# An explicit order of issue and a table of buffers in place of a planner (linear attention times an FFN gate, one core)

## The chip, the core and the metric

The kernel runs on one core of a Trainium2 chip. The metric is the device time of one execution in microseconds (us), median of the runs. A profile of one execution gives the start and the duration of every instruction on the engines: PE (TensorE; PEld is its weight load), DVE (VectorE), ACT (ScalarE), POOL (GpSimd) and SP (SyncE, which issues the DMAs), and the clock that TensorE was granted.

## The reference

```python
S, D, H, Dh, F = 2048, 512, 32, 16, 1792
xn = layernorm(x)
q, k, v = split(xn @ wqkv)                      # 32 heads of 16
phi_q = concat(softmax(q @ w_phi), softmax(-q @ w_phi))   # per head, 32 features
phi_k = concat(softmax(k @ w_phi), softmax(-k @ w_phi))
kv = einsum("bhsf,bhsd->bhfd", phi_k, v);  z = einsum("bhsf->bhf", phi_k)
o = (phi_q @ kv) / (phi_q @ z + 1e-6)
s = o @ wo
h = xn @ w1 + b1
g = silu((h * tanh(softplus(h))) @ w2)          # Dense, Mish, Dense
return x + s * g
```

## The kernel before

All data are float32. A product is done as three matmuls of a faster 4-byte type (fp32r): each operand is split into a high and a low part (names ending in h and l, as wv0h and wv0l), and low·high, high·low and high·high are summed. The large products go by a seven-product scheme for 2×2 blocks (Strassen and Winograd), so that DVE, POOL and ACT form sums of blocks of the operands ahead of the matmuls and of the products behind them.

Names that the text uses: x0 to x15 are the 16 tiles of 128 rows of the input. wkT and wqT are the transposed k and q weights, loaded in parts (wkT00, wkT01, wkT10, wkT11; wqT10, wqT00); wkf and wqf are those folded with w_phi on PE, and they go through ACT and DVE (wkh, wkl) before use. wvr0 and wvr1 are the v weights; wv0h/wv1h (ACT) and wv0l/wv1l (POOL) their parts; phic and phit the w_phi matrix. pt is a transpose of a normalised tile on PE, fh and fl its parts. kx, ky, kz, kj are products of the k and v stage; kvp the sum of phi_k·v (128 small matmuls a block); qx, qy products of the q stage; pn the numerators (115 or 116 small matmuls a block); den and f the denominators; fx, fy, fz products of the first FFN matrix (weights w1al, w1ah, w1sh and others, formed from w1a; w1b are parts that were stored to memory and are loaded again); pw the product with wo, so its result in memory; y70 to y74 and others the products of the second FFN matrix (weights w2h, w2l, w2g, w2m, w2t; operands ah, al split from r, the Mish output's blocks and sums). At the end DVE forms yc and u from y, ACT applies silu, DVE multiplies with sr (the rows of s, loaded from so) and adds xx (the rows of x, loaded again), and SP issues the stores to out.

The code does not call the engines directly. Every operation is recorded as an `Op` with its readings and writings and, for each engine that can do it, an implementation. `ORDER` is a list of parts (N4 is the norm of tile 4, wv0 the weights wv0, Fa12 a quarter of FFN block 12, Q6 a q block and so on) and fixes the order of PE's work. `Program.order` gives each operation a due time from that order, with `SHIFT` as corrections for single operations, and `Program.simulate` walks through a model of the engines with costs (`cost`), DMA rates and buffer counts, choosing for each operation when it is issued and, where several engines can do it, on which. `Program.issue` then emits everything in the order of the starts that this model gave; this is the line that carries nearly every instruction (line 404 in the kernel before, line 293 in the changed one). Each engine works off its own queue in that order, with semaphores between the engines; SP's queue is one of these, so a DMA that waits for its buffer holds those behind it.

Buffers come from pools that rotate: 8 PSUM banks, 38 slots of 4 KB per partition, 15 of tag s2, and smaller ones. Which buffer a name gets follows from the order in which the planner gives them out. For operations on POOL issued shortly after a DVE operation with two operands in SBUF, `issue` adds a dependency on it, named "port".

Of the kernel before, what the change touches and what calls it, by code (L numbers as in the profile page):

```python
# [17 lines left out]
P = 128  # L18
# [10 lines left out]
PEN, HOLD, MARGIN, GUARD = 0, 300, 1000, 140  # L29
BACK, COLD, DRATE, LANES, SWITCH = 2650, 3400, 400, 8, 230  # L30
READ, WRITE, STALL, AHEAD_PE = 1150, 150, 1500, 110
BLOCK, HEAD, FETCH, IDLE = 256, 89, 5200, 2100
BEGIN = {"PE": 1100, "V": 900, "G": 2300, "A": 800, "Q": 800}

SLOTS, S2 = 38,15
SLACK, AHEAD, LAT = 15000, 40000, 150
WAKE, EACH, NEAR = 15, 2, 4000
# [11 lines left out]
SHIFT = """  # L49
kd:0:-9100 wv1:0:-1100 N1:2:-15000 N1:3:300 N1:5:5800 N1:13:4300 N1:14:-7000 kl:3:-10000 Ka2:3:-9700 N5:6:-2200  # L50
N5:8:-1200 N5:11:13000 N2:0:-3500 N2:2:-2000 N3:4:1500 N3:13:-11400 Kc0:7:4900 Kc0:10:14200 k4:0:-6900 Kd0:6:300
N6:14:-6700 P0:1:4800 P0:5:3800 P0:11:5000 Kb1:3:300 N7:6:-2800 N7:8:7300 N7:9:-6400 N8:8:-2700 N9:13:3600 Kc1:8:1800
Kd1:4:-7300 N10:3:-300 N11:0:5800 P4:0:-7000 P4:4:300 P4:5:3100 N14:8:-6800 Kd3:1:-5000 Kd3:6:-6400 A2:0:-3600
N13:5:-2500 Fa4:1:-1100 Fa4:3:3600 N15:4:10800 N15:6:-5000 N15:11:-300 Kc5:6:4400 Ka6:1:-600 Kc6:5:-300 Kc6:6:2600
P6:6:-1100 P6:8:5100 P3:3:-2600 P3:11:-2000 Kb7:1:2800 Fa3:1:-300 Fa3:3:300 P2:4:-2000 P2:6:1100 P2:10:800 Kd6:6:-8800
Kd6:9:-9500 Fb6:3:-2300 Fc3:1:1600 Fc3:2:800 Fc3:4:7900 wQ:1:2300 wQ:13:6600 Fa2:3:300 Fa2:4:-1900 Fa1:3:900
M4:1:-1400 P5:10:3200 Q0:7:14700 Q0:23:-2000 z:4:1200 z:5:11100 D0:0:800 D0:4:4700 D0:8:-800 L:5:-4200 L:9:-3000
D1:2:-8100 Q1:16:800 Q1:19:300 Q2:3:-15000 Q2:9:-2500 Q2:15:300 Q2:25:-1900 Q3:17:-4300 Q3:18:4700 Fc5:5:9400
D3:7:1800 D4:3:-4000 D4:4:6800 D4:5:1300 D4:6:11900 D4:10:11500 D5:1:-300 Fb11:1:-4700 Q4:7:-600 Q4:16:600 Q4:18:7800
Q4:20:800 Q4:21:-1400 Q4:23:-8800 Q5:25:-600 M3:1:-5000 M3:2:-6700 Fa12:1:800 D6:6:-500 D6:10:300 Fb10:1:-500  # L60
D7:1:5000 D7:4:6600 D8:1:-2400 D8:4:-500 D8:10:1400 Q6:1:4700 D9:10:800 Q7:1:7800 Q7:16:-4700 Q7:20:4800 Q7:21:-13000
Q7:23:-12900 M2:2:-5000 D10:6:-800 M6:2:-4100 D11:1:-1700 Ua0:1:-1100 Ua0:12:-800 Fc9:1:3400 D12:5:-5000 D13:0:-4400
D13:4:12500 Fa13:4:800 Ub0:14:-4300 wo0:1:-4500 Fc13:4:-13100 Fc7:2:15000 R0:8:4700 D14:6:-7800 O3:2:-900 Ua1:2:-4200
Ua1:4:-6700 Ua1:6:-3100 Ua1:11:-5000 Ua1:13:-300 Ua1:14:300 O5:2:-500 Fd13:2:-4200 O6:1:-2200 Ub1:5:-5000 Ub1:6:-2000
Ub1:8:-4500 G7:4:-2000 R2:0:-2200 R1:1:15000 R1:6:4200 R1:10:5800 G8:3:-5000 G8:6:1900 O11:2:-2000 R6:1:4900 R3:2:1600
R3:8:-3300 R4:1:2000 G11:0:-6800 G12:5:3100 G12:6:-1200 G13:5:-1100 G32:3:6500 G34:6:4000 G1:4:-15000 G3:0:5000
G4:0:-4100 G5:5:4000 G35:3:9300 G35:4:-5800 G35:6:3100 G14:0:-10200 G14:3:4000 E0:6:-2600 G15:2:800 G39:6:-300
G16:4:-5000 G41:3:1700 E5:4:-300 G20:0:800 G20:2:-2000 G20:3:-5300 G20:6:-5000 G42:3:5100 G42:5:-300 G43:2:4200
G44:2:300 G44:4:-2000 H4:2:1300 G46:3:6600 G46:6:300 G24:6:500 G47:5:-3000 G26:4:-1600 E6:2:-800 G49:0:-5000
G49:2:4000 G49:6:-1100 G49:9:2000 G49:12:-2200 G49:19:2200 G49:26:5000 G49:31:800 G49:36:2800 G49:42:-4700 G49:43:800  # L70
E7:9:-300 E7:10:15000 H3:7:2300 H6:8:800
"""
ACT_SET = {AF.Exp: 1, AF.Silu: 3, AF.Mish: 2}


class Op:
    __slots__ = ("impl", "reads", "writes", "at", "idx", "succ", "ndep", "late", "new", "ready", "start", "eng", "sets", "slack", "open", "soon", "pos", "deps", "lock", "part", "half", "code", "tiles", "shift")


class Program:  # L80


    def __init__(self, nc):
        self.eng = {"PE": nc.tensor, "V": nc.vector, "G": nc.gpsimd, "A": nc.scalar, "Q": nc.sync}
        self.ops, self.tag, self.cap, self.pe = [], {}, {}, []
        self.group, self.slack, self.part, self.half = None, SLACK, None, False
        self.region, self.count = {}, {}
        self.shifts = {k: int(v) for k, _, v in (c.rpartition(":") for c in SHIFT.split())}

    @staticmethod  # L90
    def cost(e, m, a, k):
        aps = [v for v in a if isinstance(v, bass.AP)]
        n = aps[0].free_size()
        if e == "PE":
            if m == "transpose":
                return 109
            n, c = aps[2].free_size(), aps[1].free_size()
            if aps[1].dtype == F32R:
                return max(n / 2.4 + 0.104 * c, c * 0.835 + 2)
            full = 2 * max(n / 1.2 + 2.5, c * 0.835)  # L100
            if aps[1].shape[0] == 32:
                return max(0.155 * n, 24)
            return max(full * aps[0].shape[0] / P, 27)
        if e == "Q":
            return 450
        if e == "A":
            return (60 if aps[1].space == "PSUM" else 110) + 0.833 * n + 93 * sum(isinstance(v, bass.AP) for v in k.values())
        psum = any(v.space == "PSUM" for v in aps[1:])
        nn = max(v.free_size() for v in aps)
        if e == "V":  # L110
            if m == "reciprocal":
                return 70 + 6.3 * n
            if m in ("tensor_scalar", "tensor_copy") and not psum:
                return 70 + 0.52 * n
            return 70 + 1.04 * nn
        if k.get("op") == ALU.pow:
            return 520
        return (140 + 1.73 * n) if bcast(a) else (140 + 2.17 * n)

    @staticmethod  # L120
    def records(m, a, k):

        return 2 if m == "transpose" or a[1].dtype == F32R else 4
# [11 lines left out]
    def add(self, impl, reads, writes, sets=()):  # L135
        o = Op()
        o.tiles = {n.split("#")[0] for n in reads | writes}
        o.code = sum(self.records(*c) for c in impl["PE"][1]) if "PE" in impl else 0
        o.impl, o.reads, o.writes, o.idx, o.sets, o.slack = impl, reads, writes, len(self.ops), sets, self.slack
        o.pos, o.part, o.half = len(self.pe), self.part, self.half  # L140
        self.half = False
        key = self.part or "@"
        n = self.count[key] = self.count.get(key, -1) + 1
        o.shift = self.shifts.get(f"{key}:{n}", 0)
        o.lock = {e for e, (_, calls) in impl.items() if any(locks(e, m, a) for m, a, k in calls)}
        if "PE" in impl:
            self.pe.append(o)
        self.ops.append(o)

    def call(self, e, m, a, k):  # L150
        aps = [v for v in list(a) + list(k.values()) if isinstance(v, bass.AP)]
        w = self.names(aps[0]) - {"out"}
        r = set().union(*map(self.names, aps[1:]))
        c = self.cost(e, m, a, k)
        s = [ACT_SET[a[2]]] if e == "A" and a[2] in ACT_SET else []
        if self.group is None:
            self.add({e: (c, [(m, a, k)])}, r, w, s)
        else:
            g = self.group
            g[0].setdefault(e, [0, []])  # L160
            g[0][e][0] += c
            g[0][e][1].append((m, a, k))
            g[1].update(r)
            g[2].update(w)
            g[3].extend(s)

    def halves(self):

        self.group[0]["PE"][0] += SWITCH
        self.half = True  # L170

    @contextmanager
    def one(self):
# [4 lines left out]
        self.group = ({}, set(), set(), [])  # L178
        yield
        g, self.group = self.group, None  # L180
        self.add({e: tuple(v) for e, v in g[0].items()}, g[1], g[2], g[3])

    def order(self):
        at = [0]
        for o in self.pe:
            at.append(at[-1] + o.impl["PE"][0])
        self.links()
        return self.simulate(at)

    def links(self):  # L190
        ops = self.ops
        wr, rd, head = {}, {}, {}
        for o in ops:
            o.succ, dep = [], {head.setdefault(n, o.idx) for n in o.tiles if self.tag.get(n, "ps") != "ps"}
            for n in o.reads:
                dep.update(wr.get(n, ()))
                if self.tag.get(n) == "ps":
                    dep.update(rd.get(n, ()))
            for n in o.writes:
                dep.update(wr.get(n, ()))  # L200
                dep.update(rd.get(n, ()))
# [1038 lines left out]
```

## Time and profile before

| what | value |
|---|---|
| time, median of 3 runs | 489.14 us (489.06 to 489.71) |
| profiled execution, span | 488.7 us |
| profiled execution, whole time | not listed beside its span; the median is 0.44 us above the span |
| granted TensorE clock | 1.00 of full speed |
| PE / DVE / ACT / POOL busy | 480.2 / 446.2 / 293.4 / 267.2 us |
| DMA | 105.70 MB, mean 216 GB/s |

PE's records overlap (one begins before the last has drained), so durations of single matmuls exceed their spacing: the matmuls of 512 columns start 0.23 us apart, six of them 1.36 us, though each record shows 0.39. "Idle before" in brackets is the time in which an engine had nothing to do ahead of an instruction, and the arrow names what ended it.

### The profile page before, as it was taken

Reading aid. Unit: us, or ns where it says so; the run is one execution under the profiler, and the core shown is the slowest. Engines: PE = TensorE matmul, PEld = TensorE weight load, DVE = VectorE, ACT = ScalarE, POOL = GpSimd, SP = SyncE. Lnnn points to the kernel's source line nnn. Section 1 sums busy time; section 2 is a strip of 40 time slices with the busy share of each in tenths; the row PEclk is TensorE's granted clock in tenths of the full one; section 3 lists DMA queues with packets and bytes.
Section 4 is the critical chain, followed back from the end, with each engine's and each line's share of the span. In section 5 each row is a group of like instructions: output and inputs, shape, how many; then the busy total and the mean of one; then the engine's idle time right before and its main releaser. Section 6 shows DMA issues by size and latency. Waiting matters only on the chain.

```text
span 488.7 us, 10325 instructions
## 1 busy us (share of the span) xinstructions
PE 480.2 (98%) x3820; PEld 426.2 (87%) x3820; DVE 446.2 (91%) x893; ACT 293.4 (60%) x453; POOL 267.2 (55%) x197
## 2 busy tenths in 40 slices
PE   8899999999999999999999999999999999999996
PEld 7788888888887889898887878788899999999996
DVE  6999999988899999999999899889989889999894
ACT  3997545654556453635345545677879687777631
POOL 3989998998490446798987686370021024120030
PEclk9999999999999999999999999999999999999999
DMA  8812923968867689982959635726465646578172
GB/s 294 265 48 109 332 99 122 312 197 272 315 217 313 225 301 345 394 300 87 310 199 341 229 115 211 261 85 207 141 193 165 201 154 211 194 234 269 44 250 94
DMA packets 68641, 105.70 MB, mean 216 GB/s; under 512 B 6896, under 2 KB 37744, under 8 KB 68592
## 3 DMA queue, kind: packets, MB, share of 16 engines
q1 hardware_dynamic: 68448, 104.79, 62.9%
q8 instruction: 30, 0.49, 0.4%
q10 hardware_dynamic: 144, 0.26, 0.2%
q14 instruction: 19, 0.16, 0.1%
HBM read 60.60 MB, written 44.43 MB: 215 GB/s over the span
## 4 chain that ended last, share of the span: by engine, by line
PE 81%; DVE 8%; DMA 5%; issue 2%; ACT 1%; SPq 1%; POOL 1%; DVEq 0%; ACTq 0%
PE y L404 20%; PE fx L404 14%; PE pw L404 9%; PE kx L404 7%; PE fy L404 7%; PE qx L404 5%; PE ky L404 3%; PE fz L404 3%; PE qy L404 2%; PE kj L404 2%; PE pn L404 2%; PE kz L404 2%; DVE al L404 2%; DMA wvr<-wv 1%; DMA w1a<-w 1%
## 5 line engine op out<-in xcount | busy, mean ns | idle before, releaser
L404 POOL TENSOR_TENSOR al<-r,ah 128x896 fp32r<-128x896 f32 x8 | 17.0, 2130 | 87.4 <-DMA r<-hd 35.1
L404 ACT ACTIVATE ah<-r 128x896 fp32r<-128x896 f32 x56 | 50.9, 944 | 16.0 <-DVE r L404 12.9
L404 DVE TENSOR_TENSOR al<-r,ah 128x896 fp32r<-128x896 f32 x48 | 54.8, 1171 | 5.0 <-ACT ah L404 3.2
L404 DVE TENSOR_TENSOR r<-r 128x128 f32<-128x128 f32 (+1 forms) x157 | 48.3, 353 | 5.0 <-ACT r L404 3.4
L404 PE MATMUL y<-w2h,al 128*128 128x256 f32 x160 | 45.4, 283 | 0.0
L404 PE MATMUL y<-w2h,ah 128*128 128x256 f32 x160 | 45.3, 283 | 0.0
L404 PE MATMUL y<-w2l,ah 128*128 128x256 f32 x160 | 45.3, 283 | 0.0
L404 PE MATMUL y<-w2t,ah 128*128 128x256 f32 x224 | 41.0, 283 | 0.0
L404 PE MATMUL fx<-fh,w1b 128*128 128x512 f32 x112 | 38.8, 393 | 0.0
L404 ACT ACTIVATE r<-r 128x512 f32<-128x512 f32 x56 | 33.2, 621 | 7.9 <-DMA r<-hd 7.9
L404 PEld LDWEIGHTS y<-w2t,ah 128*128 128x128 f32 x224 | 34.9, 192 | 0.0
L404 PE MATMUL y<-w2t,al 128*128 128x256 f32 x112 | 31.7, 283 | 0.0
L404 PEld LDWEIGHTS y<-w2h,al 128*128 128x128 f32 x160 | 30.7, 192 | 0.6 <-issue 0.4
L404 PEld LDWEIGHTS y<-w2l,ah 128*128 128x128 f32 x160 | 30.7, 192 | 0.2
L404 PEld LDWEIGHTS y<-w2h,ah 128*128 128x128 f32 x160 | 30.7, 192 | 0.0
L404 PE MATMUL y<-w2g,ah 128*128 128x256 f32 x160 | 30.4, 283 | 0.0
L404 PEld LDWEIGHTS fx<-fh,w1b 128*128 128x128 f32 x112 | 21.0, 188 | 5.4 <-issue 1.2
L404 PEld LDWEIGHTS y<-w2g,ah 128*128 128x128 f32 x160 | 25.0, 192 | 0.0
L404 POOL TENSOR_TENSOR r<-r 128x128 f32<-128x128 f32 (+1 forms) x11 | 6.4, 592 | 32.3 <-DMA sr<-so 22.5
L404 PE MATMUL y<-w2g,al 128*128 128x256 f32 x80 | 22.6, 283 | 0.0
L404 ACT ACT_TABLE_LOAD x13 | 16.7, 1283 | 9.2 <-DMA x<-x 4.1
L404 PE MATMUL fx<-fl,w1b 128*128 128x512 f32 x56 | 21.8, 390 | 0.0
(766 smaller groups left out, 1730.0 us busy)
## 6 DMA issues: line engine op xcount, KB each, us to landing
r<-hd SPq DMA_DIRECT2D x56, 256.0 KB, 3.5
xd<-xc SPq DMA_DIRECT2D x8, 896.0 KB, 4.1
w1b<-w1d SPq DMA_DIRECT2D x14, 512.0 KB, 5.5
w1b<-w1d SPq DMA_DIRECT2D x14, 384.0 KB, 4.9
so<-so SPq DMA_DIRECT2D x16, 256.0 KB, 2.1
x<-x SPq DMA_DIRECT2D x15, 256.0 KB, 3.7
w1a<-w SPq DMA_DIRECT2D x7, 512.0 KB, 4.6
w1d<-w1sh SPq DMA_DIRECT2D x7, 512.0 KB, 2.9
```

The source lines that it names most:

```text
L404: ins = getattr(e, m)(*a, **k)
```

## The change

The planner (`cost`, `links`, `simulate`, the due times, `SHIFT` and all its constants) is removed. In its place stand two tables. `PLAN` names all 2455 operations, in the order in which they are issued, on all engines, PE and DMA included; an operation is its part and its number in the part, with a letter where several engines can do it (V for DVE, A for ACT, G for POOL). `PLACE` names the PSUM bank or the SBUF slot of each buffer, so the pools don't rotate: each slot is a pool entry of its own. The tables come from a search in which transfers land late at random. The "port" dependency is added where at most 24 operations, not 4000 ns of the model's time, lie between the DVE operation and the one on POOL, and not for DMAs. What is computed, and the set of instructions on PE, is the same.

```diff
-PEN, HOLD, MARGIN, GUARD = 0, 300, 1000, 140
...
-WAKE, EACH, NEAR = 15, 2, 4000
+WAKE, EACH, NEAR = 15, 2, 24
...
-SHIFT = """
-kd:0:-9100 wv1:0:-1100 N1:2:-15000 N1:3:300 N1:5:5800 N1:13:4300 N1:14:-7000 kl:3:-10000 Ka2:3:-9700 N5:6:-2200
...
+PLAN = """
+N4.0 N1.0 @.0 @.15 @.1 N4.3 @.2 @.17 @.3 N0.0 @.4 wv0.0 @.5 @.18 @.6 @.7 N4.1 @.19 @.8 @.9 N1.1 wv1.0 @.10 @.16G @.11
...
     def order(self):
+        at = {o.name: o for o in self.ops}
+        plan = []
+        for c in PLAN.split():
+            e = c[-1] if c[-1] in self.eng else ""
+            o = at.pop(c[:-1] if e else c)
+            o.eng = e or next(iter(o.impl))
+            plan.append(o)
...
     def issue(self, tc):
         first, held = True, None
-        for o in self.order():
-            for i, (m, a, k) in enumerate(o.impl[o.eng][1]):
+        for n, o in enumerate(self.order()):
+            for i, (m, a, k) in enumerate(o.impl[o.eng]):
...
-                if i == 0 and o.eng == "G" and held is not None and o.start - held[1] < NEAR:
+                if i == 0 and o.eng == "G" and m != "dma_start" and held is not None and n - held[1] < NEAR:
```

Of the 2677 rows of PE 1407 stand at the same place in both. DVE goes from 876 rows to 866, ACT from 456 to 453, POOL from 201 to 222, SP from 311 to 312. 63 operations move from DVE to POOL, 41 from POOL to DVE, 12 from ACT to DVE and 9 from DVE to ACT.

Three places follow. The first is the start of the program, on SP (the loads) and on PE. SP before:

```order
L404 DMA x4_151<-x 128x512
L404 DMA x5_153<-x 128x512
L404 DMA phic_100<-phi 128x64
L404 DMA x0_164<-x 128x512
L404 DMA wkT00_137<-wqkT 128x512
L404 DMA wkT01_138<-wqkT 128x512
L404 DMA wvr0_141<-wv 128x2x512
L404 DMA wkT10_139<-wqkT 128x512
L404 DMA wvr1_159<-wv 128x2x512
L404 DMA wkT11_140<-wqkT 128x512
```

SP after:

```order
L293 DMA x1_170<-x 128x512
L293 DMA phic_100<-phi 128x64
L293 DMA x5_153<-x 128x512
L293 DMA wkT00_137<-wqkT 128x512
L293 DMA x0_164<-x 128x512
L293 DMA wvr0_141<-wv 128x2x512
L293 DMA wkT01_138<-wqkT 128x512
L293 DMA wkT10_139<-wqkT 128x512
L293 DMA wvr1_159<-wv 128x2x512
L293 DMA wkT11_140<-wqkT 128x512
```

The same transfers stand ahead of wkT11; wkT00 and wvr0 moved forward, wkT01 back, and x1 and x4 changed places (the other of the two is the first DMA of all, on ACT's queue). PE at the same place, before (the first rows after `wake`):

```order
L404 MATMUL wkf01_147<-phit_101,wkT00_137 128x128 x4
L404 MATMUL wkf11_148<-phit_101,wkT01_138 128x128 x4
L404 MATMUL pt4_156<-ident_83,x4_151 128x128 x4
L404 MATMUL pt0_167<-ident_83,x0_164 128x128 x4
L404 MATMUL pt1_173<-ident_83,x1_170 128x128 x4
L404 MATMUL wkf21_181<-phit_101,wkT10_139 128x128 x4
L404 MATMUL wkf31_182<-phit_101,wkT11_140 128x128 x4
L404 MATMUL pt5_184<-ident_83,x5_153 128x128 x4
L404 MATMUL kx2_187<-wv0h_142,fl00_104 128x512
```

PE after:

```order
L293 MATMUL wkf01_147<-phit_101,wkT00_137 128x128 x4
L293 MATMUL pt1_173<-ident_83,x1_170 128x128 x4
L293 MATMUL pt4_156<-ident_83,x4_151 128x128 x4
L293 MATMUL wkf11_148<-phit_101,wkT01_138 128x128 x4
L293 MATMUL pt0_167<-ident_83,x0_164 128x128 x4
L293 MATMUL pt5_184<-ident_83,x5_153 128x128 x4
L293 MATMUL wkf21_181<-phit_101,wkT10_139 128x128 x4
L293 MATMUL wkf31_182<-phit_101,wkT11_140 128x128 x4
L293 MATMUL kx2_187<-wv0h_142,fl00_104 128x512
```

The transposes moved ahead of the folds of the late wkT parts. Behind kx2 (six matmuls) before come kz2 (six), wqf21, wqf31 and kj00; after come wqf21, kz2, kj00 (twelve), kj03 (six) and then wqf31.

The second place is DVE around w1al2, a part of the weights of FFN block 2. DVE before:

```order
L404 TENSOR_TENSOR w1s1_462<-w1a1_461,w1s1_462 128x256
L404 TENSOR_TENSOR k14e_475<-k14e_475,k14r_472 128x1024
L404 TENSOR_TENSOR w1s2_498<-w1a2_497 128x256
L404 TENSOR_TENSOR w1sl1_466<-w1s1_462,w1sh1_465 128x1024
L404 TENSOR_TENSOR w1al2_500<-w1a2_497,w1ah2_499 128x768
```

DVE after:

```order
L293 TENSOR_REDUCE k14m_474<-k14p_471 128x32
L293 TENSOR_TENSOR k14e_475<-k14m_474,kx7_421 128x32x16
L293 TENSOR_TENSOR w1al2_500<-w1a2_497,w1ah2_499 128x768
L293 TENSOR_REDUCE k15m_450<-k15p_446 128x32
L293 TENSOR_TENSOR k12e_460<-k12m_459,kx6_408 128x32x16
L293 TENSOR_TENSOR w1s1_462<-w1a1_461 128x256
```

w1al2 moved ahead of the sums w1s1 and w1sl1. In the order of issue its first reader on PE (fx2) came next behind it; now three groups of six matmuls come between them.

The third place is the end of DVE's queue. Before:

```order
L404 TENSOR_TENSOR yc4_1181<-yc2_1179,y71_1167 128x256
L404 TENSOR_TENSOR yc4_1181<-yc4_1181,sr13_1_1183 128x256
L404 TENSOR_TENSOR xx13_1_1182<-yc4_1181,xx13_1_1182 128x256
L404 TENSOR_TENSOR u13_0_1187<-yc2_1179,y72_1168 128x256
L404 TENSOR_TENSOR u13_0_1187<-u13_0_1187,sr13_0_1186 128x256
L404 TENSOR_TENSOR xx13_0_1185<-u13_0_1187,xx13_0_1185 128x256
L404 TENSOR_TENSOR u15_1_1190<-yc3_1180,y73_1169 128x256
L404 TENSOR_TENSOR u15_1_1190<-u15_1_1190,sr15_1_1189 128x256
L404 TENSOR_TENSOR xx15_1_1188<-u15_1_1190,xx15_1_1188 128x256
L404 TENSOR_TENSOR u15_0_1193<-u15_0_1193,sr15_0_1192 128x256
L404 TENSOR_TENSOR xx15_0_1191<-u15_0_1193,xx15_0_1191 128x256
```

After:

```order
L293 TENSOR_TENSOR u13_0_1187<-yc2_1179,y72_1168 128x256
L293 TENSOR_TENSOR u13_0_1187<-u13_0_1187,sr13_0_1186 128x256
L293 TENSOR_TENSOR yc4_1181<-yc2_1179,y71_1167 128x256
L293 TENSOR_TENSOR u15_1_1190<-yc3_1180,y73_1169 128x256
L293 TENSOR_TENSOR yc4_1181<-yc4_1181,sr13_1_1183 128x256
L293 TENSOR_TENSOR xx13_0_1185<-u13_0_1187,xx13_0_1185 128x256
L293 TENSOR_TENSOR u15_1_1190<-u15_1_1190,sr15_1_1189 128x256
L293 TENSOR_TENSOR xx13_1_1182<-yc4_1181,xx13_1_1182 128x256
L293 TENSOR_TENSOR xx15_1_1188<-u15_1_1190,xx15_1_1188 128x256
L293 TENSOR_TENSOR u15_0_1193<-u15_0_1193,sr15_0_1192 128x256
L293 TENSOR_TENSOR xx15_0_1191<-u15_0_1193,xx15_0_1191 128x256
```

u13_0 moved ahead of yc4 and its product with sr13_1. On PE the block y72 moved ahead of y70 and y71; on SP the load of sr13_1 moved from 6 rows ahead of the end to 18.

More of the change, by code (lines that the diff above doesn't have):

```diff
@@ L1 @@
 from contextlib import ExitStack, contextmanager
-import heapq
 import numpy as np
@@ L55 @@
[L55 to L59, printed above, removed]
@@ L76 @@
+"""
+PLACE = {
+    "ps": """
[4 rows of a table added]
+""",
+    "s2": """
[4 rows of a table added]
+""",
+    "slot": """
[11 rows of a table added]
+""",
+    "sm": """
[3 rows of a table added]
+""",
+    "tq": """
+1 0 1 0 0 1 0 1 0 1
+""",
+    "rq": """
+7 6 1 5 4 2 3 0 7 6 5 2 1 4 0 3
+""",
+}
 class Op:
-    __slots__ = ("impl", "reads", "writes", "at", "idx", "succ", "ndep", "late", "new", "ready", "start", "eng", "sets", "slack", "open", "soon", "pos", "deps", "lock", "part", "half", "code", "tiles", "shift")
+    __slots__ = ("impl", "reads", "writes", "idx", "name", "eng", "lock")
 class Program:
@@ L84, in __init__ @@
         self.eng = {"PE": nc.tensor, "V": nc.vector, "G": nc.gpsimd, "A": nc.scalar, "Q": nc.sync}
-        self.ops, self.tag, self.cap, self.pe = [], {}, {}, []
-        self.group, self.slack, self.part, self.half = None, SLACK, None, False
+        self.ops, self.tag = [], {}
+        self.group, self.part = None, None
         self.region, self.count = {}, {}
[L88 to L123, printed above, removed]
     def names(self, v):
@@ L133, in names, with add @@
         return {f"{n}#{where(int(e))}" for e in np.unique(at // 128) * 128}
-    def add(self, impl, reads, writes, sets=()):
+    def add(self, impl, reads, writes):
         o = Op()
[L137 to L141, printed above, removed]
         key = self.part or "@"
         n = self.count[key] = self.count.get(key, -1) + 1
[L144 to L147, printed above, removed]
+        o.impl, o.reads, o.writes, o.idx, o.name = impl, reads, writes, len(self.ops), f"{key}.{n}"
+        o.lock = {e for e, calls in impl.items() if any(locks(e, m, a) for m, a, k in calls)}
         self.ops.append(o)
@@ L408, in issue @@
             if o.eng == "V" and "V" in o.lock:
-                held = ins.ins.name, o.start + o.impl["V"][0]
+                held = ins.ins.name, n
 def locks(e, m, a):
@@ L473, in alloc @@
     def alloc(tag, shape, name, dtype=F32):
-        t = pools[tag].tile(shape, dtype, tag=tag, name=name)
+        t = pools[tag].tile(shape, dtype, tag=tag if tag == "st" else tag + next(place[tag]), name=name)
         prog.tag[t.tensor.name] = tag
```

400 lines of the change are left out of this document (143 added, 257 removed), and 22 rows, old and new, of the table PLACE.

## The prediction

> **What bounds the kernel now.** I read the page's busy line first, then the windows, the waits of PE, and the timelines of the stretches in which PE sat idle.
>
> ```profile
> PE 480.2 (98%) x3820; PEld 426.2 (87%) x3820; DVE 446.2 (91%) x893; ACT 293.4 (60%) x453; POOL 267.2 (55%) x197
> ```
>
> PE is busy for 480.2 of 488.7 us. Both kernels issue the same set of PE instructions, so reordering can only win PE's 8.5 us of idle time, or lose by making new idle time. DVE at 91% is the second bound. The windows (busy us of PE, PEld, DVE, ACT, POOL, then clock, DMA share, GB/s) say where the idle time is:
>
> ```profile
> 0.00:10.00 10.00, 8.00 (x51) 7.41 (x52) 5.70 (x22) 2.58 (x3) 3.92 (x13) 1.00 0.77 269
> 10.00:20.00 10.00, 8.39 (x57) 7.11 (x57) 9.34 (x23) 9.00 (x20) 8.30 (x5) 1.00 0.97 305
> 20.00:140.00 120.00, 120.00 (x799) 99.73 (x799) 109.84 (x210) 76.12 (x120) 106.01 (x78) 1.00 0.59 201
> 140.00:160.00 20.00, 19.73 (x325) 15.96 (x324) 19.97 (x27) 12.15 (x17) 6.00 (x4) 1.00 0.78 286
> 260.00:280.00 20.00, 20.00 (x205) 15.89 (x204) 18.41 (x45) 9.77 (x18) 13.01 (x9) 1.00 0.79 278
> 280.00:300.00 20.00, 20.00 (x205) 15.89 (x204) 19.23 (x42) 11.34 (x21) 15.37 (x11) 1.00 0.52 184
> 300.00:320.00 20.00, 20.00 (x296) 15.50 (x296) 17.66 (x32) 11.90 (x23) 10.06 (x12) 1.00 0.59 201
> 475.00:488.70 13.70, 9.13 (x77) 8.93 (x75) 5.84 (x14) 1.52 (x4) 0.00 (x0) 1.00 0.36 126
> ```
>
> PE is idle for 2.00 and 1.61 us in the first two rows, 0.27 us at 140 to 160, 4.57 us in the tail, and nowhere else. The clock is 1.00 throughout. The waits of PE name the releasers:
>
> ```profile
> PE wake L404 <- DVE mhalf L527: 1.1, 1, 1.1
> PE wkf L404 <- DMA wkT<-wqkT: 1.0, 2, 0.7
> PE wqf L404 <- ACT wqf L404: 0.7, 1, 0.7
> PE pt L404 <- DVE x L404: 0.6, 2, 0.4
> PE fx L404 <- DVE w1al L404: 0.3, 1, 0.3
> PE kz L404 <- POOL wv1l L404: 0.2, 1, 0.2
> ```
>
> The wait of `wake` is the program's start and stays. The rest, 2.8 us, is what a better order of issue can address; the tail comes on top.
>
> **The start.** In PE's timeline (start, duration, then the group) and, in the last two lines, POOL's and ACT's:
>
> ```profile
> 10.81 1.13 PE L404 MATMUL wkf<-phit,wkT 128*128 128x128 f32 x8
> 12.67 1.16 PE L404 MATMUL wkf<-phit,wkT 128*128 128x128 f32 x8 [0.73 <-DMA wkT<-wqkT]
> 13.66 0.60 PE L404 MATMUL pt<-ident,x 128*128 128x128 f32 x4
> 14.02 0.48 PE L404 MATMUL kx<-wv0h,fl 128*128 128x512 f32 x1
> 15.47 0.39 PE L404 MATMUL kz<-wv1h,fl 128*128 128x512 f32 x1
> 16.06 0.50 PE L404 MATMUL kz<-wv1l,fh 128*128 128x512 f32 x1 [0.20 <-POOL wv1l L404]
> 17.32 1.05 PE L404 MATMUL wqf<-phit,wqT 128*128 128x128 f32 x8
> 19.06 1.16 PE L404 MATMUL wqf<-phit,wqT 128*128 128x128 f32 x8 [0.69 <-ACT wqf L404]
> 19.97 0.48 PE L404 MATMUL kj<-wv0h,fl 128*128 128x512 f32 x1
> 13.60 2.40 POOL L404 TENSOR_TENSOR wv1l<-wvr,wv1h 128x1024 fp32r<-128x1024 f32 x1
> 12.10 1.07 ACT L404 ACTIVATE wv1h<-wvr 128x1024 fp32r<-128x1024 f32 x1
> ```
>
> The fourth wkf (wkf31) starts when wkT11 lands, about 12.6. In SP's new order the loads issued ahead of wkT11 are the same ones, in another sequence (x0 and wvr0 have moved ahead of wkT01, x1 and x4 have swapped queues), so I keep 12.67. From there the new PE order is wkf31, kx (6), wqf21, kz (6), kj00, with pt5 already done during the wait and wqf31 put off. From the starts above, wkf takes 13.66 − 12.67 = 0.99, kx 15.47 − 14.02 = 1.45 and wqf about 19.97 − 19.06 = 0.91. That puts kz at 12.67 + 0.99 + 1.45 + 0.91 = 16.02, wv1l being needed one matmul later, at 16.25. POOL finished it at 16.00 before; now it is no later, since wvr0 is loaded ahead of wkT01 and ACT's wv1h has the same place. With kz at 1.36 (the usual six, below) and 0.1 for the return from a wqf, kj00 starts at 17.5. One wqf (0.91) is still owed, so equal work stands at 18.4 against 19.97: **−1.6 us**. The two recovered waits (0.69, 0.20), pt5's 0.36 out of the path, and the gap in kz's row (16.06 − 15.47 − 0.23 = 0.36) account for most of it. I put the bounds at −0.8 (wkT11 or wv1l later by about the 0.73 that wkf waited before) and −2.4 (wkT11 earlier by as much).
>
> **Passages between kinds of matmul.** The chain of waits shows what follows a block of small matmuls:
>
> ```profile
> 38.38 1.36 PE ky L404 x6
> 102.72 1.93 PE kvp L404 x128
> 104.65 1.59 PE kx L404 x6
> ```
>
> Six large matmuls behind kvp take 1.59 where the usual six take 1.36: 0.23 for a passage. In the order of issue the returns from kvp/pn go from 7 to 8 and those from wkf/wqf from 1 to 4, those from pt from 9 to 8. The first costs +0.23; a return from wqf or pt costs the 0.09 by which kx takes 1.45 and not 1.36, so +0.27 − 0.09. Together +0.4, of which 0.2 is already in the start (the 1.45 and the 0.1): **+0.2 us**. Ends: 0 (PE catches up at the next wait) and 0.6.
>
> **The wait for w1al.** At 150 us PE's fx waited 0.3 us for DVE's w1al2. In PLAN three groups of six matmuls (4.1 us at 1.36) stand between w1al2 and its first reader, where there was none: **−0.3 us**; ends −0.4 and 0 (DVE, busy 19.97 of 20 there, is late with the next thing).
>
> **The tail.** DVE's last rows, and ACT's last:
>
> ```profile
> 480.99 0.43 DVE L404 TENSOR_TENSOR yc<-yc,sr 128x256 f32<-128x256 f32 x1 [3.17 <-DMA sr<-so]
> 484.85 0.42 DVE L404 TENSOR_TENSOR xx<-u,xx 128x256 f32<-128x256 f32 x1
> 485.19 0.42 DVE L404 TENSOR_TENSOR u<-u,sr 128x256 f32<-128x256 f32 x1
> 485.65 0.42 DVE L404 TENSOR_TENSOR xx<-u,xx 128x256 f32<-128x256 f32 x1
> 484.27 0.36 ACT L404 ACTIVATE u<-y 128x256 f32<-128x256 f32 x1
> ```
>
> The last u·sr could start at 484.27 + 0.36 + 0.03 = 484.66, but DVE is late with its queue until 485.19, since one block waited 3.17 us for the load of sr13_1. In the new SP order this load stands 18 rows from the end instead of 6, and y72 is computed before y71, so that u13_0 leaves the queue before the last two y blocks are ready. Six DVE operations of about 0.42 are left behind the last but one y block, and PE's last block takes 21 × 0.12 = 2.5 us: they just fit. **−0.5 us**; ends −0.55 and 0.
>
> **DVE and POOL.** 63 operations leave DVE for POOL and 41 come the other way, 7 of the 8 `al` of POOL among the latter. I priced both lists with the mean of each form's group: DVE gains about 7 us over the kernel, POOL loses 10, ACT 0.7. I cost this at nothing, since PE waits once for DVE outside the start; the cover is DVE's idle time, and the thin place is 260 to 320 us. There the new DVE list has about 8 us more ahead of the same PE matmuls, while DVE's idle time in the three rows is 1.59 + 0.77 + 2.34 = 4.7 us. So what is uncovered is between 0 (a list that runs ahead earlier pays it before 260) and 3.3 us. I take 0, because up to 260 the new list stands level with the old one or ahead of it, and in 20:140 DVE has 10 us of idle time and never held PE. Rows on how DVE and POOL meet:
>
> ```profile
> L404 DVE TENSOR_TENSOR al<-r,ah x48: 1079/1085/3228, 312.8 to 463.1; 128x896 fp32r<-128x896 f32 x48
> L404 POOL TENSOR_TENSOR al<-r,ah x8: 2121/2130/2137, 363.9 to 464.4; 128x896 fp32r<-128x896 f32 x8
> L404 POOL TENSOR_TENSOR r<-r x11: 454/508/751, 308.5 to 436.1; 128x128 f32<-128x128 f32 x6, 128x256 f32<-128x256 f32 x5
> ```
>
> The longest `al` on DVE is 3.228 us, its usual 1.085 plus one POOL `al` (2.13). The Trainium skill, page "SBUF — State Buffer", section "SBUF: two separate sides", calls the port pair that the two engines share an exclusive lock: whichever starts first holds it for the whole instruction and the other fully blocks. The row agrees with it (3.23 against 1.09 + 2.13). By that rule the short `r` that now go to POOL would block DVE more often and for shorter. In rows: 22 more POOL operations at 0.508 us are 11.2 us of POOL time; if a quarter of it stopped a DVE operation, DVE would lose 2.8 us, and the seven `al` that leave POOL give back up to 2.13 each. So I leave it out of the sum.
>
> **The sum.** −1.6 + 0.2 − 0.3 − 0.5 = −2.2 us on a span of 488.7, so 486.5. The median of the runs, 489.14, is 0.44 above this span, which I take as the time around it: **486.9 us**.
>
> **The rivals.**
> - *The start isn't moved* (no change): wkT11 and wv1l land as much later as wkf waited before (0.73), and the wait takes back the start. Against it: the loads ahead are the same. 489.14 − 0.3 − 0.5 + 0.2 = 488.5.
> - *DVE becomes the bound at 260 to 320 us* (no change to slower): if 2.2 us of the 3.3 are uncovered the whole gain is gone, and PE shows waits for den, f or ol. With the full 3.3 it gives 486.9 + 3.3 = 490.2. It decides from 3.2 us on. For it: DVE at 19.23 of 20 in 280 to 300. Against it: the windows on either side have room.
> - *A reload comes late* (slower): w1b35, a part of the first FFN matrix, now goes into the buffer that the last qx/qy products of Q6 read, and stands ten rows behind its sister w1b25 in SP's queue, not directly behind. From the last reader to its first use PE has four groups of 1.36 and some qx/qy, about 6.2 us.
>
> ```profile
> DMA to landing us min/median/max: 2.9/5.3/9.2
> ```
>
>  This row is w1b's loads from issue to landing. At the median of 5.3 it is in time; at 9.2 PE waits 3.0 us: 489.9. It is slower than no change from a landing of 9.4 on, and takes the gain from 8.4.
> - *More than summed*: the start at −2.4 and nothing paid for passages: 485.9.
>
> **How the numbers follow.** About 0.2% (1 us) is what a measurement of this kernel can tell from no change. Chances: the forecast 0.48 (own range 486.2 to 487.9); more than summed 0.14; the start not moved 0.12, in the same band; DVE 0.16, half of it in the band and half above; the late reload 0.10, half and half. Faster is thus 0.62 and a little of the start's case, 0.64; same 0.22; slower 0.14. The range leaves out about one in ten on each side: from 485.6 (below the largest gain) to 490.0 (most of DVE's and the reload's).
>
> **What would show it.** Right: PE's windows 0:20 idle for about 2 us instead of 3.6, kj00's first row near 17.5, no wait of wqf for ACT; no fx waiting for w1al; DVE's last u·sr straight behind ACT's last u; PE at 20.00 of 20 from 20 to 475 us. Wrong: rows in PE's waits with DVE den, f, ol or w2 between 260 and 330, or fx waiting for DMA w1b near 250; wkf waiting over 1.4 us for wkT in all. What would make the prediction wrong most easily is DVE: its list is longer, and I have only bounded how that meets PE.

## The result and the profile after

The changed kernel takes 485.82 us (median of 4 runs, 485.75 to 486.15) against 489.25 us (4 runs, 489.06 to 489.71): a ratio of 0.9932, 95% interval 0.9918 to 0.9946. It is 3.4 us faster; the forecast was 486.9, that is 2.2 us faster.

The page's busy line after:

```profile
PE 478.1 (99%) x3820; PEld 426.1 (88%) x3820; DVE 444.5 (92%) x874; ACT 286.7 (59%) x450; POOL 262.7 (54%) x219
```

PE does the same 3820 matmuls in 2.1 us less "busy" time. Busy time thus contained waits; the reading beforehand had missed this. The windows (columns as before) and PE's waits:

```profile
0.00:10.00 10.00, 7.87 (x49) 7.62 (x50) 5.75 (x22) 3.22 (x5) 3.99 (x13) 1.00 0.83 289
10.00:20.00 10.00, 10.00 (x65) 8.93 (x64) 9.90 (x26) 8.78 (x20) 9.15 (x6) 1.00 1.09 379
140.00:160.00 20.00, 20.00 (x213) 16.78 (x212) 19.39 (x25) 10.69 (x16) 6.85 (x8) 1.00 0.77 255
260.00:280.00 20.00, 20.00 (x213) 15.62 (x216) 19.14 (x43) 12.23 (x22) 13.93 (x9) 1.00 0.73 252
280.00:300.00 20.00, 20.00 (x205) 16.09 (x205) 19.41 (x44) 8.96 (x20) 13.73 (x11) 1.00 0.66 232
300.00:320.00 20.00, 20.00 (x331) 15.70 (x330) 18.63 (x40) 12.99 (x28) 7.49 (x10) 1.00 0.52 178
```

```profile
PE wake L293 <- DVE mhalf L394: 1.1, 1, 1.1
PE pt L293 <- DVE rs L293: 1.0, 1, 1.0
```

The waits of wkf, wqf, kz and fx are gone; pt waits once for the norm. PE is never idle from 10 to 475 us, although DVE is fuller than before between 260 and 320 us (57.2 us busy against 55.3). The start and the end in the timeline after:

```profile
9.19 0.66 PE L293 MATMUL pt<-ident,x 128*128 128x128 f32 x4 [1.01 <-DVE rs L293]
11.52 1.95 PE L293 MATMUL wkf<-phit,wkT 128*128 128x128 f32 x16
13.22 0.48 PE L293 MATMUL kx<-wv0h,fl 128*128 128x512 f32 x1
15.51 0.48 PE L293 MATMUL kz<-wv1h,fl 128*128 128x512 f32 x1
16.97 0.39 PE L293 MATMUL kj<-wv0h,fl 128*128 128x512 f32 x1
480.25 0.38 ACT L293 ACTIVATE u<-y 128x256 f32<-128x256 f32 x1 [1.57 <-PE y L293]
480.67 0.43 DVE L293 TENSOR_TENSOR u<-u,sr 128x256 f32<-128x256 f32 x1 [0.63 <-ACT u L293]
```

kj00 starts at 16.97, with one wqf (0.91) still owed: equal work stands at 17.9 against 19.97. At the end DVE now waits for ACT, not the other way about: its last product starts 0.04 us behind ACT's last u.

**Hidden waits.** A matmul's record lasts longer than the spacing to the next one, so a wait shorter than the overlap leaves no gap and isn't counted as idle. In PE's timeline of the kernel before, at the last product of a q block (the last line is DVE's):

```profile
167.41 0.28 PE L404 MATMUL qy<-wqs1l,fh 128*128 128x256 f32 x1
167.53 0.28 PE L404 MATMUL qy<-wqs1h,fh 128*128 128x256 f32 x1
167.68 0.39 PE L404 MATMUL qx<-wq1h,fl 128*128 128x256 f32 x1
167.90 0.28 PE L404 MATMUL qx<-wq1l,fh 128*128 128x256 f32 x1
167.20 0.42 DVE L404 TENSOR_TENSOR q1p<-q1p,qx 128x256 f32<-128x256 f32 x1
```

The usual spacing is 0.12 us; here it is 0.15 and 0.22, with no bracket. Each q block writes the bank qx four times (a running sum), and between the third write and the fourth stand only the six short matmuls of qy (0.72 us). The last line shows DVE reading the third result until 167.62; the fourth write starts at 167.68. To see such waits I summed, from the starts, how far each step between neighbouring matmuls exceeds the median step of its kind (shorter steps count against it). Passages between kinds of matmul are in these sums too, so only the differences between the columns tell of waits:

| stretch, us | before | before as tables (c0_tables) | after |
|---|---|---|---|
| 0 to 21 | 2.73 | 1.84 | 0.51 |
| 21 to 162 | 5.96 | 5.52 | 5.36 |
| 162 to 260 | 1.58 | 1.54 | 0.51 |
| 260 to the end | 3.40 | 3.41 | 3.39 |

Eleven steps of the q blocks are too long by about 0.1 us before; none is after, where other products stand between those of a q block. With the idle time of the windows taken off, the 2.1 us that busy time fell by are about 1.1 us in the q blocks, 0.7 in the start and 0.3 between 21 and 162 us.

**The span and the time.** The profiled execution shown beforehand had a span of 488.7 us. In all later runs the time lies 1.7 to 2.1 us above the span (1.67 in the profiled run of the changed kernel: 485.87 against 484.2), so that execution was, by estimate, one of about 490.6 us (488.7 + 1.9) and slower than the median, not 0.44 faster. The runs of the kernel before spread over 1.4 us (488.43 to 489.84 in 18 runs on one chip). The difference of the spans 488.7 and 484.2 is therefore not the gain. What lies around the span goes with the engines and not with the order: 1.67 to 1.80 us where all or nearly all operations stand on the new engines (c0_letters below included), 1.88 to 1.99 in c0_tables, e_q_spread, l_before and after_letters with the old ones. What it consists of isn't shown.

### The profile page after: what moved, and what is told of

It is laid out like the page before. It is cut to its first block, busy times and chain, and to the rows that moved or that the text cites. A ratio compares the mean times of both kernels' runs of the same rounds, so it can differ in the third digit from the quotient of the medians.

```text
span 484.2 us, 10225 instructions
## 1 busy us (share of the span) xinstructions
PE 478.1 (99%) x3820; PEld 426.1 (88%) x3820; DVE 444.5 (92%) x874; ACT 286.7 (59%) x450; POOL 262.7 (54%) x219
## 4 chain that ended last, share of the span: by engine, by line
PE 97%; DVE 1%; DMA 1%; POOL 0%; ACT 0%; issue 0%
PE y L293 29%; PE fx L293 16%; PE pw L293 9%; PE fy L293 8%; PE kx L293 8%; PE qx L293 5%; PE ky L293 4%; PE fz L293 4%; PE qy L293 2%; PE kj L293 2%; PE pn L293 2%; PE kz L293 2%; PE kvp L293 2%; PE pt L293 1%; PE qz L293 1%; PE wqf L293 1%
## 5 line engine op out<-in xcount | busy, mean ns | idle before, releaser
L293 POOL TENSOR_TENSOR r<-r 128x128 f32<-128x128 f32 (+1 forms) x40 | 24.5, 626 | 90.8 <-DVE al L293 30.5
L293 DVE TENSOR_TENSOR al<-r,ah 128x896 fp32r<-128x896 f32 x55 | 59.3, 1094 | 8.0 <-PE y L293 3.5
L293 ACT ACTIVATE ah<-r 128x896 fp32r<-128x896 f32 x56 | 52.4, 947 | 21.2 <-PE y L293 7.7
L293 PE MATMUL y<-w2t,ah 128*128 128x256 f32 x224 | 42.3, 283 | 0.0
L293 DVE TENSOR_TENSOR r<-r 128x128 f32<-128x128 f32 (+1 forms) x128 | 39.6, 354 | 1.3 <-POOL r L293 1.2
L293 PE MATMUL y<-w2g,ah 128*128 128x256 f32 x160 | 31.6, 283 | 0.0
L293 PEld LDWEIGHTS y<-w2t,al 128*128 128x128 f32 x112 | 21.5, 192 | 0.0
L293 POOL TENSOR_TENSOR sr<-yy,sr 128x512 f32<-128x512 f32 x3 | 3.8, 1293 | 29.3 <-DVE al L293 25.9
```

What stands on the lines that cost most here:

```text
L293: ins = getattr(e, m)(*a, **k)
```

## The experiments

The first four ask whether the gain is in the order, and in which stretch. All kernels below are the changed file with other tables (nearly every instruction then stands at line 296). A prefix of one order is always complete in what it depends on, so the orders can be joined: the first operations from one, all others in the sequence of the other, with buffers given accordingly. The joined kernels (h_start, h_q, h_oldstart) thus have a table of buffers of their own, and what they lose is put down to the order only where the trace names the wait.

**c0_tables**: order, engines and buffers of before, written as tables.

```diff
-N4.0 N1.0 @.0 @.15 @.1 N4.3 @.2 @.17 ...   (PLAN and PLACE of the changed kernel)
+N1.0 @.0 @.1 N4.0 @.2 @.3 ...              (those that the planner gave before)
```

> The order and the buffers of the kernel before, written as the two tables. Theory (the gain is in the order: a few waits of PE that go away, each at its place): 489.2 us, within 0.5 of the kernel before, PE with the same waits (wkf, wqf, pt, fx, kz) and 11 steps of about 0.1 us too long among the q products. Rival (the form of the tables gains: fixed slots and the port rule by count of operations): faster by 1 to 3.4 us. The span will also show whether the time around it is 0.4 us or the 1.65 of the changed kernel (485.87 against a span of 484.2).

489.23 us (11 runs), ratio to before 1.0004 (0.9996 to 1.0013): the form of the tables, with fixed slots and the new rule for "port", is neither here nor there. Its 11 long q steps are the same as before's, and in its faster execution (488.71, span 486.8) PE waits less for loads:

```profile
PE wqf L296 <- ACT wqf L296: 0.7, 1, 0.7
PE pt L296 <- DVE x L296: 0.4, 1, 0.4
PE kz L296 <- POOL wv1l L296: 0.2, 1, 0.2
```

The wait of 1.0 us for wkT isn't there: wkT11 landed at 11.73 us, against 12.62 in the execution shown beforehand, with the same queue. It belonged to the execution and not to the kernel.

**h_start**: the new start, the rest as before.

```diff
-PLAN = all 2455 operations in the new order
+PLAN = new order [0:198] + order of before without these 198
```

> The first 198 operations in the new order (the start, until the four products kj are issued, on all engines), all the others in the order of before. Theory (local waits): the start's 2.2 us and nothing else, so 487.0, with fx still waiting for w1al at 148 and the long q steps still there. Rival (the gain hangs on the whole order, DVE being the second bound): an earlier start is taken back by DVE later, new waits of PE appear between 20 and 320 us, and the time is 488.5 to 489.2.

491.62 us, ratio 1.006 (1.0046 to 1.0075): slower than before by 2.7 us. The theory fell. The start did win (0.91 us of excess in 0 to 21 instead of 1.84), but 3.5 us were lost at 31 to 48 us: 1.0 in a transpose that waits for ACT's x, 1.8 in a wait for DVE's k3p. Rows of PE, DVE, POOL and ACT on the second, then the same places in c0_tables:

```profile
48.04 0.47 PE L296 MATMUL kx<-wkh,fl 128*128 128x512 f32 x1 [1.80 <-DVE k3p L296]
43.95 0.42 DVE L296 TENSOR_TENSOR xs<-xr,pt 128x256 f32<-128x256 f32 x1 [2.57 <-POOL w1s L296]
31.32 1.83 POOL L296 TENSOR_TENSOR w1al<-w1a,w1ah 128x768 fp32r<-128x768 f32 x1
41.43 1.06 POOL L296 TENSOR_TENSOR k0e<-k0m,k0p 128x512 f32<-128x512 f32 x1
42.52 1.06 ACT L296 ACTIVATE k0e<-k0e 128x1024 f32<-128x1024 f32 x1 [2.19 <-POOL k0e L296]
43.49 0.37 ACT L296 ACTIVATE xr<-pt 128x256 f32<-128x256 f32 x1
```

```profile
40.36 1.86 POOL L296 TENSOR_TENSOR w1al<-w1a,w1ah 128x768 fp32r<-128x768 f32 x1
37.95 1.06 POOL L296 TENSOR_TENSOR k0e<-k0m,k0p 128x512 f32<-128x512 f32 x1
40.96 0.42 DVE L296 TENSOR_TENSOR xs<-xr,pt 128x256 f32<-128x256 f32 x1 [0.20 <-ACT xr L296]
```

The new head issues things early that the old order did late. POOL has w1al at 31.3 instead of 40.4, ahead of k0e and not behind it, and k0e starts at 41.43 instead of 37.95 (w1al's 1.83 us are about half of that). ACT's exponential of k0e waits 2.19 us for it, and xr stands behind that in ACT's queue. DVE's xs reads xr and pt, not w1s: the bracket names POOL's w1s, which ended at 43.88, but ACT's xr ended at 43.86, and in c0_tables the same row waits for ACT's xr. So DVE, whose queue goes in order, stands 2.57 us for xr; k3p is late, and PE waits 1.80 us. That chain through three queues, and not DVE's total load, is what the trace shows for this wait. In the changed kernel DVE does this part of k0e itself, so that k0e doesn't wait for POOL there.

**h_q**: the new order through the q products.

```diff
+PLAN = new order [0:1278] + order of before without these 1278
```

> The first 1278 operations in the new order (through all q products, about 262 us), the rest in the order of before. Theory (local waits): start -2.2, w1al -0.43, passages -0.15, q steps -1.1, so 485.4 by the span's count (less what lies around the span, if that grew); the rest as before with a DVE wait of 3 us in the tail. Rival (the second half of the new order matters too, by the exchange of operations between DVE and POOL): above 486.5, with PE waits after 262 us.

490.54 us, ratio 1.0033 (1.0021 to 1.0045). Up to 260 us its excess is that of the changed kernel within 0.15 us in each stretch; behind the seam PE waits again, so the time says nothing of the second half by itself:

```profile
PE fz L296 <- DVE hb L296: 1.4, 1, 1.4
PE pn L296 <- DVE ol L296: 0.6, 1, 0.6
```

**e_q_spread**: the last q product of each block put off.

```diff
 (order of before as tables, for n = 0 to 7)
-... Qn.12 ... <next PE operation>
+... <next PE operation> Qn.12 ...
```

> The kernel before as tables, with the last product on the bank qx of each of the 8 q blocks put off behind the next PE operation (six matmuls), so that its bank is read out for 0.7 to 1.4 us longer before it is written again. Theory (the long steps in the q blocks are waits for DVE to read the bank, hidden from the idle time because matmul records overlap): 8 of the 11 long steps go, PE's busy time falls by about 0.8 us, time 488.4. Rival (the long step is a fixed cost of a matmul that carries a semaphore wait): the steps stay, 489.2.

490.54 us, ratio 1.0034 (1.0022 to 1.0046). In the trace the theory holds: all 8 long steps at wq1h are gone, the matmul now following in step. PE at one of these places, and then the wait that came instead:

```profile
167.88 0.39 PE L296 MATMUL fx<-fh,w1ah 128*128 128x512 f32 x1
168.10 0.28 PE L296 MATMUL qx<-wq1h,fl 128*128 128x256 f32 x1
168.22 0.28 PE L296 MATMUL qx<-wq1l,fh 128*128 128x256 f32 x1
172.49 0.50 PE L296 MATMUL pz<-zaccl,oner 128*128 128x512 f32 x1 [0.77 <-DVE zaccl L296]
```

So the long step is a wait for the bank and not a fixed cost. The time theory failed: DVE's and ACT's readers of the delayed product hold their queues, pz waits 0.77 us for zaccl, and other q products get long steps (the excess in 162 to 260 us is 2.45 against 1.54). These 0.9 us are over half of the 1.6 us by which its profiled span exceeds that of c0_tables; 0.4 more is the start, with a wkT11 that landed late (12.47). A wait removed in one place in an order that is otherwise full came back elsewhere, larger.

**h_oldstart**: the mirror of h_start.

```diff
+PLAN = order of before [0:198] + new order without these 198
```

> The mirror of h_start: the first 198 operations in the order of before, all the others in the new order. Theory after h_start (an order is timed as a whole: DVE's list only fits a PE that comes at the time for which it was laid out, but a PE that comes later than that finds everything ready): no new waits of PE between 20 and 320 us, so the changed kernel plus the start's 1.3 to 2.2 us, 487.1 to 488.0, with runs spread by about 1.4 us as those of before, since the start waits for its loads again. Rival (each seam between the two orders costs, whichever way): new waits of PE of 1 us or more behind the seam, 489 or above.

487.54 us (487.04 to 488.88, 11 runs), ratio 0.9969 (0.996 to 0.9978), as expected. No wait of PE behind the seam, only those of the start:

```profile
PE wkf L296 <- DMA wkT<-wqkT: 1.7, 1, 1.7
PE wqf L296 <- ACT wqf L296: 0.7, 1, 0.7
```

This parts the gain: the rest of the new order is worth 1.6 us (487.54 against 489.13 on the same chip), and the new start 1.7 us more (485.82, measured in another group of runs; the two intervals of the ratio don't meet). The runs are again spread by 1.8 us.

**after_letters and c0_letters**: the engines exchanged without the order.

```diff
 (new order, engines of before; and the reverse)
-... N1.6V ... N5.1A ...
+... N1.6A ... N5.1V ...     (125 letters in each)
```

> The new order and buffers, but every operation on the engine that did it before (125 operations change engine, among them 63 from POOL back to DVE and 41 back to POOL). Theory (the engines were chosen together with the order; the exchange is neither here nor there by itself, DVE 7 us lighter and POOL 10 us heavier again, but in the new order the long al stand on POOL where their products are soon wanted): waits of PE for al or den, 486.5 to 489. Rival A (the exchange gains nothing): 485.8 as the changed kernel. Rival B (the exchange of DVE and POOL is where the gain lies): 489 or more.

500.55 us, ratio 1.023 (1.0216 to 1.0244).

> The counterpart: order and buffers of before, every operation on the engine that does it in the changed kernel. Theory (order and engines belong together): slower than before, 489.5 to 493, by DVE, which has 7 us more to do in an order that had no room for it between 140 and 160 us and around 260 to 320 us. Rival (the exchange itself gains, by shorter blocking of DVE by POOL): 486 to 488.

509.44 us, ratio 1.0415 (1.0399 to 1.0431). Both are far slower than either kernel, and by more than expected. The time of after_letters alone lies where its rival B had it; c0_letters refutes that rival, since the exchange without the order loses 20 us. In the new order with the old engines the largest waits of PE are for al, first of all those that went back to POOL; in the old order with the new engines DVE waits 16 times for the r that went to POOL:

```profile
PE y L296 <- POOL al L296: 2.8, 3, 1.4
PE y L296 <- DVE al L296: 1.9, 3, 1.2
```

```profile
DVE r L296 <- POOL r L296: 13.8, 16, 1.8
```

Order and engine were one choice. The waits shown for PE are 4.7 of the 14.7 us that after_letters loses; the rest, and how much of DVE's 13.8 us reaches PE in c0_letters, was not followed up.

**t_undo**: the tail of before in the changed kernel.

```diff
-E3.2 E7.6 E7.11 ... H3.4 H3.7G G49.54 E7.2 H3.8G E7.3 E7.13 E7.14 E7.15 E7.4 ...
+E3.2 E7.11 ... H3.4 E7.6 H3.7G G49.54 E7.2 H3.8G E7.3 E7.4 E7.7 E7.8 E7.9 ... E7.13 E7.14 E7.15 ...
```

> The changed kernel with the tail of before: sr13_1 is loaded behind the store of xx7, and DVE does yc4 with sr13_1 and xx13_1 ahead of u13_0, as before. Theory (the tail's 0.5 us comes from these two together): DVE waits for sr13_1 and its last product starts 0.3 to 0.8 us behind ACT's last u instead of 0.04, time 486.3 (+0.5). Rival (the tail is bound by PE's last block and the store alone): 485.8, no change.

487.0 us (486.29 to 487.25), ratio 0.9951: 1.2 us more than the changed kernel, where 0.5 was expected. PE ends at the same time to 0.01 us; the whole loss is in DVE's queue:

```profile
477.71 0.43 DVE L296 TENSOR_TENSOR yc<-yc,sr 128x256 f32<-128x256 f32 x1 [1.30 <-DMA sr<-so]
481.05 0.36 ACT L296 ACTIVATE u<-y 128x256 f32<-128x256 f32 x1
481.98 0.42 DVE L296 TENSOR_TENSOR u<-u,sr 128x256 f32<-128x256 f32 x1
```

ACT's last u is late too, 481.05 against 480.25, since the u ahead of it waits for DVE. In c0_tables the same tail cost nothing (DVE's last product 0.04 us behind ACT's u), in the execution shown beforehand 0.56. What it costs goes with how long before PE's end sr13_1 lands: 3.85 us in c0_tables, 3.23 in the execution shown beforehand, 2.58 in t_undo (landing at 477.62, PE's end at 480.20).

**s_newdma and s_olddma**: is it the loads or PE's order that makes the start faster? The first 14 loads exchanged:

```diff
 s_newdma: h_oldstart with the new sequence of loads
-N1.0 N4.0 N4.3 @.15 N0.0 @.17 @.18 wv0.0 @.19 wv1.0 @.20 N2.0 wq1.0 N2.3
+N4.0 N1.0 @.15 N4.3 @.17 N0.0 wv0.0 @.18 @.19 wv1.0 @.20 wq1.0 N2.0 N2.3
 s_olddma: the changed kernel, the reverse
```

> h_oldstart (the start in the order of before, the rest new) with the 14 first loads in the new sequence: x4 first on ACT's queue, x1, phic and wkT00 early, wvr0 ahead of wkT01. Theory (the start's gain lies in PE's order, with the transposes ahead of the wkT parts that land late; the loads alone don't help a PE that asks for wkT01 second): within 0.5 of h_oldstart (487.54), and the runs as spread as there. Rival (the sequence of loads gives the start's 1.7 us): about 486.

487.84 us, against 487.54 for h_oldstart: nothing won. PE asks for wkT01 second, and that is now loaded behind wvr0:

```profile
9.29 1.16 PE L296 MATMUL wkf<-phit,wkT 128*128 128x128 f32 x8 [1.38 <-DMA wkT<-wqkT]
```

> The changed kernel with the first 14 loads in the sequence of before. Theory (PE's order gives the gain): 485.8 to 486.6, since wkT11 lands as before and PE has the transposes to do meanwhile. Rival (the sequence of loads gives it): 487 to 487.5, with PE waiting for x1 or wvr0, which now come later than the new PE order asks for them.

486.49 us, ratio 0.9952 (0.994 to 0.9964): by the medians 1.05 of the start's 1.7 us stays with the old loads, 0.7 goes. By the traces the split is even: the excess in 0 to 21 us is 1.14, against 1.84 in c0_tables and 0.51 after. The interval meets that of h_oldstart and that of the changed kernel, so no more can be said than that PE's order gives half of it or somewhat more, and that the loads add the rest only together with that order.

**l_before and l_after**: does the new order stand a late transfer better?

```diff
 (both kernels, on SP; wkT11 is @.20, x2, x3, x6 are N2.0, N2.3, N6.0)
-... wv1.0 @.20 ... N2.0 ... N2.3 ... N6.0
+... wv1.0 N2.0 N2.3 N6.0 @.20 ...
```

> The kernel before as tables, with the loads of x2, x3 and x6 put ahead of that of wkT11, so that wkT11 lands 1.9 us later (three transfers of 0.63 us each by the landings). Theory (the order of before has no slack at this load): all of it is paid, 489.1 + 1.9 = 491.0, PE waiting for wkT some 1.9 us more. Rival (the load was early enough): 489.1.

490.52 us, 1.4 us more than before by the medians; the ratio is 1.0039 (1.0025 to 1.0052), that is 1.2 to 2.5 us, which holds the expected 1.9.

> The same delay in the changed kernel. Theory (the new order has about 1.0 us between wkT11's landing at 11.4 and its first matmul at 12.4, which is what lets it stand late transfers): 0.9 of the 1.9 us is paid, 486.7, and less in what follows, since x2 and x3 are there earlier. Rival A (no slack): 487.7. Rival B (slack enough): 485.8.

487.36 us, ratio 0.9969 (0.9958 to 0.998), 1.5 us more than the changed kernel. PE's wait for wkT11 in l_before and in l_after:

```profile
13.86 1.16 PE L296 MATMUL wkf<-phit,wkT 128*128 128x128 f32 x8 [1.78 <-DMA wkT<-wqkT]
```

```profile
13.61 1.13 PE L296 MATMUL wkf<-phit,wkT 128*128 128x128 f32 x8 [0.71 <-DMA wkT<-wqkT]
```

wkT11 landed 2.1 us later in both (13.81 against 11.73, 13.47 against 11.40). The new order's slack of 0.9 us is there in the trace, the old order has none at this load, and yet both end 1.4 to 1.5 us later. The start alone pays 1.6 us in the old order (there the delay gives back part, for instance the wait of kz for wv1l) and 1.26 in the new one, which loses 0.3 more behind 260 us. The expected 0.9 was too little. By the totals the new order isn't better protected against this one late load.

The traces say more on the start itself. Here is the landing of wkT11 in ten of them, with the excess of PE's steps in 0 to 21 us:

| start | run | wkT11 lands, us | excess, us |
|---|---|---|---|
| before's | c0_tables | 11.73 | 1.84 |
| before's | e_q_spread | 12.47 | 2.28 |
| before's | before | 12.62 | 2.73 |
| before's | h_oldstart | 12.64 | 2.79 |
| before's | l_before | 13.81 | 3.45 |
| new | h_q | 11.27 | 0.53 |
| new | t_undo | 11.30 | 0.56 |
| new | after | 11.40 | 0.51 |
| new | h_start | 12.50 | 0.91 |
| new | l_after | 13.47 | 1.77 |

With the old start a landing 0.9 us later costs up to 0.95; with the new one 1.1 us later costs 0.4. The new start is thus worth 1.3 us when wkT11 lands early and 1.4 to 1.9 when it lands at about 12.5. These are single executions in which other loads moved as well. That the runs of the changed kernel were closer together (0.4 us in 4 runs) isn't shown to be its property: t_undo, with the same start, has 1.0 us in 5 runs.

## Why the prediction was right, and where it was off

- **Start (−1.6).** The size agrees with h_oldstart's −1.7, in part by luck. The starting point was an execution with a late wkT11 (12.62), and the sum kept that landing; in the changed kernel's trace it landed at 11.40, and kj00 came at 16.97 for a forecast 17.5. Against the execution shown the traces differ by 2.22 us, against c0_tables' by 1.33, and 1.6 lies between. The landing is no property of the order: with one and the same queue it came between 11.73 and 12.64 us.
- **The cause of the start.** The sum followed PE's order and took the loads as unchanged in effect. s_newdma and s_olddma bear out the first and correct the second: about 0.7 us of it comes from the loads, with the new PE order.
- **Passages (+0.2).** With w1al the stretch of 21 to 162 us fell by 0.16 us against c0_tables, where the step at w1al was 0.22 too long: about +0.06 is left. The direction can't be told at this size.
- **w1al (−0.3).** Gone, 0.2 to 0.43 by the step. Right.
- **Tail (−0.5).** Right against the execution shown (0.6), and nothing against c0_tables' (0.05). Undoing it cost 1.2: in t_undo PE ends 2.57 us earlier than in c0_tables, the load lands only 1.31 earlier.
- **DVE and POOL (0).** Right in the outcome: no wait of PE between 260 and 320 us. The sizes behind it were wrong. DVE was priced 7 us heavier over the kernel and 8 at 260 to 320 us; its busy time fell by 1.7 (446.2 to 444.5) and grew by 1.9 there. One reason is in the prices: the mean of DVE's al, 1171 ns for a usual 1085, held 4.1 us of waits over 48 of them, nearly all in two; after, it is 1094. The cover by idle time was too weak a reason too: after_letters and c0_letters show that the same exchange in another order costs 14.7 and 20 us. The lists were fitted to each other, which a sum of loads doesn't show.
- **The longest al.** The al of 3.23 us was read as blocked by an al on POOL, since 1.09 + 2.13 happens to fit. It stood beside POOL's w2l; the second longest, 3.00 us at 366.05, stood beside an al.

```profile
326.46 3.23 DVE L404 TENSOR_TENSOR al<-r,ah 128x896 fp32r<-128x896 f32 x1
326.34 2.39 POOL L404 TENSOR_TENSOR w2l<-w2r,w2h 128x1024 fp32r<-128x1024 f32 x1 [0.43 <-DVE w2m L404]
```

  Both al ended 0.95 us after the operation on POOL, so that the blocking was read rightly and the blocker not: two of POOL's three w2l went to DVE as well as seven of its eight al.
- **What was missing: the q blocks.** The step that failed is the first, "can only win PE's 8.5 us of idle time". In the q blocks 1.03 to 1.07 us of waits stood inside the busy time, and the new order took nearly all of it; this term is missing from the sum. The Trainium skill, page "Perfetto Trace Analysis", section "Matmuls", says that independent groups of matmuls should rotate through PSUM banks so that reading one out overlaps the next. The trace agrees as to the reason (11 long steps where the same bank came back after 0.72 us), but here the bank holds a running sum, and other work in between did it, not another bank.
- **The span.** The 0.44 us around it was wrong; it is 1.7 to 2.1. It made no difference to the predicted time, since the difference was taken from the median.
- **The reload of w1b35** did not come late; PE has no wait there. Its rival's price wasn't tried.

Together, by the traces of c0_tables and the changed kernel: 1.33 (start) + 1.03 (q blocks) + 0.16 (w1al and passages) = 2.5 of the 2.6 us between the spans (486.8 and 484.2). The medians lie 0.8 us farther apart than these spans: 0.24 of it lies outside the spans (1.91 against 1.67), and c0_tables' profiled execution was among its fastest (488.71, median 489.23: 0.5). That slower executions of before pay for loads that land later is what the traces of the old start show above; how much of these 0.5 us falls on the start and how much on the tail stays open.

## What to carry to other kernels

Look at the steps from start to start of the bounding engine, not at its idle time alone: overlapping records hide waits shorter than the overlap, and here those of the q blocks were about a third of the gain. Don't take a part of a searched order by itself: the new start, the new engines, or one postponed product per q block each made the old order slower, while the new rest bore an old start without harm. And read several executions before a wait for a load is counted as the kernel's: its landing moved by up to 0.9 us from one to the next. A bracket's releaser is inferred, too: ask whether the operation reads what is named.

## What the runs showed of the hardware

- The same 11 first loads in the same queues brought wkT11 between 11.73 and 12.64 us (c0_tables, e_q_spread, before, h_oldstart). A pause in the landings stood at another place from one to another: 3.01 us ahead of wvr0 (7.10 to 10.11, before), 1.90 ahead of x0 (5.11 to 7.01, e_q_spread), where neighbours land 0.65 us apart for 256 KB and 1.3 for the 512 KB of a wvr.
- A PE matmul that had to wait for a PSUM bank, if only briefly, starts its successor 0.22 us later instead of 0.12 (8 of the 11 steps; 0.20 in the other three), also where no idle time is recorded.
- Two engines that pass small tiles to each other pay for it in DVE's queue where the order doesn't allow for it: in c0_letters DVE waited 13.8 us in 16 waits for r on POOL, in the changed kernel, with 40 such operations, 1.2 us in 2.
- The three al on DVE that were longest beside an operation on POOL, which had started first, each ended 0.95 us after it: 329.69 after 328.74 (w2l, before), 369.05 after 368.10 (al, before), 420.41 after 419.46 (r, after). So the length goes with what POOL had left: the longest al is 3.23 us before and 1.35 after (usual 1.09).
